# Delta-rule attention, Mish block and Sinkhorn experts on one core: block 0 solved by 16x16 triangles with TensorE products, block 1 solved on VectorE late in the Mish units

## The chip, the cores and the metric

One NeuronCore of a Trainium2 chip runs the whole program. The metric is the device time of one execution in microseconds (us), the median of several runs. All times below are us unless marked ns. TensorE (PE) multiplies, VectorE (DVE), ScalarE (ACT) and GpSimd (POOL) work element by element, SyncE (SP) issues the transfers.

## The reference

Three stages follow one another; `_moe_ref` and `_moe2_ref` are a Mish block and eight experts.

```python
for t in range(S):                                  # S = 768, batch 4, 8 heads, D = 48
    kt, vt, bt = (k_n[:, :, t], v[:, :, t], beta[:, :, t, None])
    y[:, :, t] = np.einsum('bhd,bhde->bhe', q[:, :, t], state)
    v_old = np.einsum('bhde,bhd->bhe', state, kt)
    state = state + bt[:, :, :, None] * np.einsum('bhd,bhe->bhde', kt, vt - v_old)
...
h = x @ w_in; sp = log1p(exp(h)); g = h * tanh(sp); x = g @ w_out      # d_ff = 2048
...
P = exp(x @ w_gate - max)                           # then 8 Sinkhorn rounds over rows and columns
out += P[:, e:e + 1] * (np.maximum(x @ w1[e], 0.0) @ w2[e])            # e = 0..7, F = 1024
```

## The kernel before, in words

The sequence is cut into 6 blocks of 128 steps (`NBLK`), each block into two chunks of 64. Inside a chunk the recurrence is a triangular system: with G the masked product of the keys among themselves, every head needs the inverse of a unit triangular 64x64 matrix. The kernel inverts the two 32x32 diagonal triangles of each and joins them with TensorE products:

- `st_gk`, `st_gq`, `st_g` (lines 988 to 1035) multiply keys with keys and keys with queries. `mask_g` and `causal` mask what `st_g` copied out unmasked.
- `lane_in_one` or `lane_in_ops` turns the triangles by 32x32 transposes into the tile `lane`, where every partition holds a triangle of its own; `elim_ops` (line 1075) eliminates there in 30 steps, each one product (line 1083) and one addition (line 1089) on up to 240 elements of a partition. `st_lane_out` (line 1097) transposes the result twice, into `t11` and `diag`.
- `st_place`, `st_m1` and `st_m2` put the inverted triangles back into `gx` and make the 32x32 corner between them, by 64 products each.
- The chain of the block is then `st_z`, `st_w`, `st_s`, `st_y` for each of its two chunks, two at a time; `st_x1` transposes its result into the input of the Mish block.

Before the first Mish unit there is a head: all of this for block 0, with nothing to hide it, and the raw products of block 1. Then come the windows, one for a block: 16 Mish units, and in windows 0 and 1 the 8 units of expert 0 after them. Mish unit f is `m_first` (9 products of 512 columns, line 300), Mish on ACT (`m_a`, line 1289), a split into a high and a low part (`m_c`; the low part `gl` on DVE, line 1299) and `m_second` (9 products, line 1310). A bank that `m_first` wrote is free again when `gl` has been made. In window 0 the weights are also decoded from 64-bit numbers: a transfer (`fetch`, lines 167 and 171), a scaling on ACT (line 206), three instructions on DVE (lines 189, 192, 197), a split on ACT (line 260) and a subtraction on DVE (line 262) for each unit; the transfer for unit i+4 is issued when unit i is converted, and a copy of each converted unit is stored to memory.

The order on every engine is the order of the program text (`manual_schedule`). What stands beside which unit comes from the table `PLACES`: for block c+1 the mark at which its solve must be finished (`drain_elim`, `st_lane_out`; `st_m1` follows one mark later, `st_place` and `st_m2` two), the marks of its chain stages; and for block c+2 the marks of its norms, masks, `st_g` and the start of its solve. Marks 0 to 15 are the Mish units, 16 to 19 the end of the Mish part (f1 to f4), 20 to 27 expert 0. `fill(us)` takes solve steps worth so many planned us from the queue `eq` after each unit.

Block 0 is solved in the head by all 60 instructions of `elim_ops`. Block 1's solve begins at the end of the head: 18 instructions on POOL (`elim1(18, nc.gpsimd)`), the other 42 on DVE beside Mish units 3 to 11, and its chain stands at marks 14 to 22.

Of the kernel before, what the change touches and what calls it, by code (L numbers as in the profile page):

```python
# [84 lines left out]
def delta_mish_sinkhorn_kernel(  # L85
# [691 lines left out]
    def o_store():  # L777

        u, half, t = todo.popleft()
        if t < 0:  # L780
            f, x, (n, d) = fin[u], slice(512 * half, 512 * half + 512), divmod(~t, KD)
            tt(out=f[:, d, x], in0=f[:, d, x], in1=f[:, 3 + 3 * n + d, x], op=ALU.add)
            return
            return True
        o_write(u, half, t, o_turn(u, half, t, (0, 1, 2)))

    todo = deque()
# [8 lines left out]
    if True:  # L796
# [9 lines left out]
        lane = ap_p.tile([128, 32, 32], F32, name="lane")  # L806
# [22 lines left out]
        def gx(c):  # L829
            return gxs[c % 2]  # L830
# [236 lines left out]
        def lane_in_one(c):  # L1067
            v = gx(c).rearrange("p t h x -> p x (t h)")
            return [
                (1.94, lambda: nc.vector.transpose(out=lane, in_=v[:, 0:32, :])),  # L1070
                (0.09, lambda: nc.vector.memset(lane.rearrange("p t i -> p (t i)")[:, 0:1024:33], 1.0)),
                (0.0, lambda: diag_clear(c)),
            ]

        def elim_ops(c, eng=(nc.vector,)):
            ops = []
            for s in range(1, 31):
                n = 31 - s
# [278 lines left out]
        with tc.manual_schedule():  # L1357
# [44 lines left out]
            for _, op in lane_in_one(0):  # L1402
                op()
            e0 = [op for _, op in elim_ops(0)]

            def el(n):
                for _ in range(n):
                    e0.pop(0)()
# [9 lines left out]
            banks[:] = [0, [A1, A1, (ps_o1, "o0")]]  # L1418
            for t in range(4):
                run(*[lambda hf=hf: st_g(1, t, hf, False) for hf in range(2)])  # L1420
            for n in range(4):
                begin_decode(n)
            el(len(e0) - 24)
            nc.vector.memset(mi_f[1][:, 0:1], 0.0)
            warm(12, i=1)
            el(len(e0))
            st_lane_out(0)

# [4 lines left out]
            def elim1(n, eng):
                elim_eng[0] = eng
                for _ in range(min(n, len(ops1))):
                    ops1.popleft()[1]()
# [9 lines left out]
            for op in norm_ops(1, ALL):
                op()
            for t in range(4):
                prep_mb(1, t, nc.gpsimd)
            for t in range(4):  # L1450
                mask_g(1, t, nc.gpsimd)
# [7 lines left out]
            for t in range(2, 4):  # L1459
                prep_v_act(0, t)  # L1460
            s0[0]()
            s0[1]()
            converts(1)
            z1 = [st_z(0, t) for t in range(2, 4)]
            z1[0]()
            gq[0]()
            z1[1]()
            gq[1]()
            run(*[lambda t=t: st_y(0, t) for t in range(2)])
            for n in range(4, 6):  # L1470
                fetch(n)
            for t in range(4):
                diag_left(1, t)
            in1 = [op for _, op in lane_in_one(1)]
            elim_eng = [nc.gpsimd]
            ops1 = deque(elim_ops(1, elim_eng))
            dec(2)
            wb = [st_w(0, t) for t in range(2, 4)]
            gq[2]()
            wb[0]()  # L1480
            gq[3]()
            wb[1]()
            run(*[lambda t=t: st_y(0, t) for t in range(2, 4)])
            for n in range(6, 8):
                fetch(n)
# [26 lines left out]
        def drain_decode():  # L1512
# [11 lines left out]
        def window(c):  # L1524
# [53 lines left out]
        with tc.manual_schedule():  # L1578
            banks[:] = [0, [A1, A1]]
            for c in range(NBLK):  # L1580
# [36 lines left out]
                for f in range(U1 + (3 if c < NE0 else 2)):  # L1617
# [240 lines left out]
```

## Time and profile before

| what | us |
| --- | --- |
| median of 3 runs | 2233.88 |
| the runs | 2229.70, 2234.07, 2233.88 |
| the profiled execution, its own time | 2229.53 |
| span of its trace, first to last instruction | 2227.7 |
| mean granted clock of TensorE in it | 0.978 of 2.4 GHz |

The span leaves 1.8 us outside the trace. All starts below count from the start of the span. In the views a line such as `L1083` is a line of the kernel before; `x64` counts instructions, and an fp32 product counts as two of them (two passes); what stands in brackets is how long the engine stood idle before, and what ended it.

### The profile page before, as it was taken

Reading aid. Unit: us, or ns where it says so; the run is one execution under the profiler, and the core shown is the slowest. Engines: PE = TensorE matmul, PEld = TensorE weight load, DVE = VectorE, ACT = ScalarE, POOL = GpSimd, SP = SyncE. Lnnn points to the kernel's source line nnn. Section 1 sums busy time; section 2 is a strip of 40 time slices with the busy share of each in tenths; the row PEclk is TensorE's granted clock in tenths of the full one; section 3 lists DMA queues with packets and bytes.
Section 4 is the critical chain, followed back from the end, with each engine's and each line's share of the span. In section 5 each row is a group of like instructions: output and inputs, shape, how many; then the busy total and the mean of one; then the engine's idle time right before and its main releaser. Section 6 shows DMA issues by size and latency. Waiting matters only on the chain.

```text
span 2227.7 us, 34746 instructions
## 1 busy us (share of the span) xinstructions
PE 2165.4 (97%) x14133; PEld 1792.0 (80%) x14133; DVE 1394.4 (63%) x2289; ACT 691.9 (31%) x1212; POOL 673.6 (30%) x528
## 2 busy tenths in 40 slices
PE   7889898999999999999999999999999999999999
PEld 6668787888888788888888888888888888888887
DVE  8894726473821276777776776666666666666665
ACT  6453332333324445233333322112212121211122
POOL 3504441435324656677878600000000000000000
PEclk7799999999999999999999999999999999999999
DMA  6576733544446446655555444444443454444441
GB/s 185 184 245 202 232 124 133 191 165 154 143 143 207 161 156 221 233 195 199 202 195 197 153 143 155 150 148 161 138 161 124 150 154 158 137 147 147 165 151 43
DMA packets 123648, 370.35 MB, mean 166 GB/s; under 512 B 9440, under 2 KB 51232, under 8 KB 123232
## 3 DMA queue, kind: packets, MB, share of 16 engines
q1 hardware_dynamic: 122912, 367.74, 48.3%
q8 instruction: 111, 1.82, 0.3%
q10 hardware_dynamic: 576, 0.39, 0.1%
q14 instruction: 49, 0.40, 0.1%
HBM read 274.15 MB, written 93.95 MB: 165 GB/s over the span
## 4 chain that ended last, share of the span: by engine, by line
PE 86%; DVE 8%; issue 2%; DMA 1%; POOL 1%; ACT 1%; SPq 0%; DVEq 0%; POOLq 0%; ACTq 0%
PE s L663 33%; PE b L596 31%; PE psh L300 7%; PE x L1310 6%; DVE t L1083 1%; DVE lane L1089 1%; PE y L324 1%; PE psa L1020 1%; DVE us L876 1%; PE psa L1168 1%; DVE lane L1053 1%; PE psa L1126 1%; PE psa L1141 1%; PE psa L1224 1%; PE psa L1190 1%
## 5 line engine op out<-in xcount | busy, mean ns | idle before, releaser
L596 PE MATMUL b<-gx,gw 128*128 128x512 f32 x3036 | 795.5, 390 | 0.1
L603 DVE TENSOR_TENSOR gt<-b,gt 128x512 f32<-128x512 f32 x644 | 436.0, 689 | 460.8 <-PE b L596 429.5
L596 PEld LDWEIGHTS b<-gx,gw 128*128 128x128 f32 x3036 | 568.5, 188 | 118.6 <-ACT gt L605 0.9
L663 PE MATMUL s<-gh,gw 128*128 128x512 f32 x2208 | 622.7, 390 | 0.6 <-DVE gy L706 0.4
L638 ACT ACTIVATE gh<-gt 128x512 fp32r<-128x512 f32 x368 | 232.8, 633 | 933.5 <-DVE gt L632 926.1
L663 PEld LDWEIGHTS s<-gh,gw 128*128 128x128 f32 x2208 | 413.6, 188 | 87.0 <-DVE gy L706 0.8
L663 PE MATMUL s<-gl,gw 128*128 128x512 f32 x1104 | 326.8, 390 | 0.0
L632 DVE SCALAR_TENSOR_TENSOR gt<-gt,gp 128x512 f32<-128x512 f32 x336 | 277.0, 825 | 4.5
L300 PE MATMUL psh<-x,w 128*128 128x512 f32 x1008 | 262.0, 405 | 11.8 <-DVE gl L1299 10.1
L663 PEld LDWEIGHTS s<-gl,gw 128*128 128x128 f32 x1104 | 206.8, 188 | 42.8
L300 PEld LDWEIGHTS psh<-x,w 128*128 128x128 f32 x1008 | 188.2, 192 | 59.8 <-DVE gl L1299 9.5
L641 POOL TENSOR_TENSOR gl<-gt,gh 128x512 fp32r<-128x512 f32 x128 | 186.3, 1462 | 77.4 <-ACT gh L638 72.3
L641 DVE TENSOR_TENSOR gl<-gt,gh 128x512 fp32r<-128x512 f32 x240 | 164.5, 686 | 37.0 <-ACT gh L638 36.8
L1299 POOL TENSOR_TENSOR gl<-x,gh 128x512 fp32r<-128x512 f32 x80 | 103.0, 1288 | 256.1 <-ACT gh L1297 238.5
L536 POOL TENSOR_TENSOR gx<-gxr,gx 128x768 fp32r<-128x768 f32 x18 | 33.3, 1847 | 407.0 <-ACT gx L535 407.0
L1310 PE MATMUL x<-gh,w 128*128 128x512 f32 x576 | 155.3, 406 | 0.0
L467 POOL TENSOR_TENSOR gw<-gr,gw 128x640 fp32r<-128x640 f32 x70 | 117.5, 1680 | 68.2 <-ACT gw L477 66.4
L1310 PEld LDWEIGHTS x<-gh,w 128*128 128x128 f32 x576 | 109.4, 194 | 24.0 <-issue 1.4
L1291 ACT ACTIVATE x<-psh 128x512 f32<-128x512 f32 x80 | 47.7, 596 | 132.3 <-PE psh L300 123.3
L1310 PE MATMUL x<-gl,w 128*128 128x512 f32 x288 | 82.8, 396 | 2.3 <-POOL gl L1299 2.3
L467 POOL TENSOR_TENSOR gw<-raw,gw 128x384 fp32r<-128x384 f32 x70 | 73.3, 1068 | 7.3 <-ACT gw L499 7.3
L984 POOL TENSOR_TENSOR kq<-kq,mask_sb 64x256 f32<-64x256 f32 (+1 forms) x72 | 58.6, 814 | 55.0 <-ACT kq L979 51.2
(203 smaller groups left out, 1984.8 us busy)
## 6 DMA issues: line engine op xcount, KB each, us to landing
gw<-wg SPq DMA_DIRECT2D x57, 1280.0 KB, 8.1
w<-wd SPq DMA_DIRECT2D x88, 768.0 KB, 4.4
gw<-wg SPq DMA_DIRECT2D x57, 768.0 KB, 5.1
wg<-gw SPq DMA_DIRECT2D x29, 1280.0 KB, 6.0
wg<-gw SPq DMA_DIRECT2D x29, 768.0 KB, 5.3
wd<-w SPq DMA_DIRECT2D x24, 768.0 KB, 5.7
gr<-in_w_dram SPq DMA_DIRECT2D x35, 384.0 KB, 3.2
raw<-in_w_dram SPq DMA_DIRECT2D x35, 384.0 KB, 3.8
```

What stands on the lines that cost most here:

```text
L300: mm(ps, lhsT=wi(u, pw, kc), rhs=(xh, xl)[px][:, kc, :], start=(n == 0), stop=(n == 3 * KD - 1))
L467: nc.gpsimd.tensor_tensor(out=w[:, 1, lo:hi], in0=r, in1=w[:, 0, lo:hi].bitcast(F32), op=ALU.subtract)
L596: mm(ps, lhsT=w[:, pw, i * 128:i * 128 + 128], rhs=x[:, px, j, :], start=(n == 0), stop=(n == last))
L603: add = lambda o, i: nc.vector.tensor_tensor(out=t[:, o], in0=ps, in1=t[:, i], op=ALU.add)
L632: nc.vector.scalar_tensor_tensor(out=t, in0=t, scalar=0.0, in1=pbs[u, e][:, o:o + 512], op0=ALU.max, op1=ALU.mult)
L638: nc.scalar.activation(out=h, in_=t, func=AF.Copy)
L641: return lambda: eng.tensor_tensor(out=l, in0=t, in1=h.bitcast(F32), op=ALU.subtract)
L663: mm(o[k], lhsT=w[:, pw, at:at + 128], rhs=hids[s, z][ph], start=(start and new and n == 0), stop=(end and not new and n == 2))
L984: nc.gpsimd.tensor_tensor(out=o, in0=o, in1=mask_sb[p, None, :].to_broadcast([64, hs.stop - hs.start, CH]), op=ALU.mult)
L1291: nc.scalar.activation(out=mi_x[u % 2], in_=hps.pop(u), func=AF.Mish)
L1299: eng.tensor_tensor(out=l, in0=p, in1=h.bitcast(F32), op=ALU.subtract)
L1310: mm(x2ps[c][k], lhsT=wo(u, pw, k * 128, k * 128 + 128), rhs=(h, l)[pg], start=(f == 0 and n == 0), stop=(f == U1 - 1 and n == 2))
```

## The change

- Block 0: `half_ops` eliminates the 16x16 diagonal triangles of each 32x32 triangle, both in one instruction (`lane2` is a view of them), 14 steps of two instructions on 28 to 112 elements, after POOL has cleared the square between them. `st_e16` and `st_o16` make that square by TensorE products with 16 rows and 16 columns (128 products, then 192), with ACT copies and six DVE additions between and behind them.
- The raw products of block 1 (`raw_g`, one call for half the heads of a 64-step chunk) no longer stand before block 0's inverse, but in eight pieces between the stages of its chain. The masked copies of `st_gq` (DVE) move ahead of the chain, `diag_left(1, t)` on ACT behind it.
- Block 1 is solved wholly on DVE: queued at Mish unit 11, 0.6 us of fill up to there and 3.4 from unit 12 on, finished at mark 17; its chain stands at marks 20 to 27, beside expert 0. Block 2's solve is queued at mark 27 instead of 26, one mask at 24 instead of 23 and the last at 25 instead of 24.

```diff
+        lanes = ap_p.tile([128, 1056], F32, name="lane")
+        lane = lanes[:, 0:1024].rearrange("p (t i) -> p t i", i=32)
+        lane2 = lanes.rearrange("p (k m) -> p k m", k=2)[:, :, 0:512].rearrange("p k (t i) -> p k t i", i=32)
...
+        def half_ops(c):
+            t = t11.rearrange("p b i -> p (b i)")
+            ops = [(0.0, lambda: nc.gpsimd.memset(lane[:, 16:32, 0:16], 0.0))]
+            for s in range(1, 15):
+                n = 15 - s
+                p = t[:, 0:2 * n * s].rearrange("p (k n s) -> p k n s", k=2, s=s)
...
+                        out=p, in0=lane2[:, :, s + 1:16, s:s + 1].to_broadcast([128, 2, n, s]),
+                        in1=lane2[:, :, s:s + 1, 0:s].to_broadcast([128, 2, n, s]), op=ALU.mult,
...
+        def st_e16(c, hf):
...
+                    mm(ps[p:p + 32, i], lhsT=g[p:p + 16, t, h, o:o + 32], rhs=t11[p:p + 16, t * H + h, :],
+                       start=True, stop=True)
+            return lambda: nc.scalar.activation(out=em(hf), in_=ps, func=AF.Copy, scale=low16)
+        def st_o16(c, hf):
...
+                    mm(ps[q, 0, i], lhsT=diag[q, b, :], rhs=e[q, i, 0:16], start=True, stop=True)
...
+                    mm(ps[q, 1, i], lhsT=e[q, i, :], rhs=diag[q, b, 16:32], start=True, stop=True)
...
-            for t in range(4):
-                run(*[lambda hf=hf: st_g(1, t, hf, False) for hf in range(2)])
...
+            raw_g((0, 0))
+            el(12)
             nc.vector.memset(mi_f[1][:, 0:1], 0.0)
-            warm(12, i=1)
+            warm(10, i=1)
             el(len(e0))
             st_lane_out(0)
...
+            ea, eb = st_e16(0, 0), st_e16(0, 1)
+            ea()
+            eb()
+            gq[0]()
+            oa, ob = st_o16(0, 0), st_o16(0, 1)
...
+            raw_g((0, 1))
...
+            oa()
+            gq[3]()
+            ob()
             m1a = m_run(st_m1(0, 0, (32,)))
...
-            elim1(18, nc.gpsimd)
...
-            (11, two(14, 15, 17, 18, 19, 20, 21, 22), 16, [21, 22, 23, 24], two(23, 24, 25, 26), 18, 26, 26),
+            (17, two(20, 21, 22, 23, 24, 25, 26, 27), 16, [21, 22, 24, 25], two(23, 24, 25, 26), 18, 26, 27),
...
-                rest["s3"].append(lambda: eq.extend(ops1))
+                rest["s11"].append(lambda: eq.extend(elim_ops(1)))
...
-                    fill(1.2 if not c else 3.2 if c >= NE0 and f > 8 else 2.0)
+                    fill((0.6 if f < 12 else 3.4) if not c else 3.2 if c >= NE0 and f > 8 else 2.0)
```

Three places show the new order. The first is ACT at the end of the head, where block 0's result `yd` becomes the Mish input `x`. Before:

```order
L1226 ACTIVATE yd<-psa 128x384 x2
L1061 ACTIVATE gx_153<-gx_153 32x8x32 x8
L1226 ACTIVATE yd<-psa 128x384 x2
L260 ACTIVATE w_90<-bits_174 128x768
L1234 ACTIVATE x_1107<-psa 128x512 x3
```

and with the change (lines of the changed kernel: 1286 is `st_y`, 981 the copies of `st_g`, 1063 `diag_left`, 1294 `st_x1`):

```order
L1286 ACTIVATE yd<-psa 128x384 x2
L981 ACTIVATE gx_153<-psa 128x256
L981 ACTIVATE kq_147<-psa 64x256 x2
L981 ACTIVATE gx_153<-psa 128x256
L981 ACTIVATE kq_147<-psa 64x256 x2
L206 ACTIVATE xr<-xr 128x768
L206 ACTIVATE bits_175<-bits_175 128x768
L1286 ACTIVATE yd<-psa 128x384 x2
L1063 ACTIVATE gx_153<-gx_153 32x8x32 x8
L260 ACTIVATE w_90<-bits_174 128x768
L1294 ACTIVATE x_1409<-psa 128x512 x3
```

The eight copies of `diag_left` moved from between the two pairs of `yd` to behind the last one, and copies of block 1 and two scalings moved in between.

The second is DVE in a Mish unit of window 0 (`gl` is line 1299, `lane` and `t` are the solve). Before, one unit late in the decoding:

```order
L1299 TENSOR_TENSOR gl<-psh,gh 128x512
L1089 TENSOR_TENSOR lane<-lane,t_167 128x11x20
L1083 TENSOR_TENSOR t_167<-lane 128x210
L1089 TENSOR_TENSOR lane<-lane,t_167 128x10x21
L189 TENSOR_SCALAR kq_141<-kq_141 128x768
L192 SCALAR_TENSOR_TENSOR kq_141<-kq_141 128x768
L197 SCALAR_TENSOR_TENSOR kq_141<-kq_141 128x768
L262 TENSOR_TENSOR w_89<-kq_140,w_89 128x768
```

With the change the same unit runs from its `gl` straight into the decoding, and the solve (lines 1085 and 1091) begins behind the `gl` of unit 10:

```order
L1359 TENSOR_TENSOR gl<-psh,gh 128x512
L1085 TENSOR_TENSOR t_167<-lane 128x30
L1091 TENSOR_TENSOR lane<-lane,t_167 128x30
L1085 TENSOR_TENSOR t_167<-lane 128x58
L189 TENSOR_SCALAR kq_142<-kq_142 128x768
L192 SCALAR_TENSOR_TENSOR kq_142<-kq_142 128x768
L197 SCALAR_TENSOR_TENSOR kq_142<-kq_142 128x768
L262 TENSOR_TENSOR w_90<-kq_141,w_90 128x768
L1359 TENSOR_TENSOR gl<-psh,gh 128x512
L1091 TENSOR_TENSOR lane<-lane,t_167 128x29x2
```

Eleven solve instructions follow this second `gl` (unit 11), then nine, eight, eight and nine behind those of units 12 to 15, and the rest among the last steps of the Mish part; 42 had stood beside units 3 to 11 before.

The third is PE where block 1's inverse is used (`gx_153`). Before, `st_m1` stood between the first products of unit 13 and the second ones of unit 11:

```order
L300 MATMUL psh<-x_1107,w_89 128x512 x2
L300 MATMUL psh<-x_1108,w_89 128x512
L1126 MATMUL psa<-t_167,gx_153 32x32 x64
L1310 MATMUL x_1255<-gh,w_93 128x512
L1310 MATMUL x_1256<-gh,w_93 128x512
```

With the change it follows the second products of the last unit, 15, and nothing stands between (1186 is `st_m1`, 1201 `st_m2`, 1228 and 1229 `st_z`):

```order
L1370 MATMUL x_1540<-gl,w_92 128x512
L1370 MATMUL x_1541<-gl,w_92 128x512
L1186 MATMUL psa<-t_167,gx_153 32x32 x64
L1201 MATMUL psa<-yd,mb_176 32x32 x32
L1201 MATMUL psa<-yd,mb_177 32x32 x32
L1228 MATMUL psa<-us_162,kq_144 64x48
L1229 MATMUL psa<-us_162,kq_144 64x48
```

`st_m1`, `st_m2` and the first chain stage moved as one piece from among the Mish units to between them and expert 0.

## Rows read from the trace of the kernel before

**Rows 1.** The page: busy shares, and the chain that ended last by engine.

```profile
PE 2165.4 (97%) x14133; PEld 1792.0 (80%) x14133; DVE 1394.4 (63%) x2289; ACT 691.9 (31%) x1212; POOL 673.6 (30%) x528
PE 86%; DVE 8%; issue 2%; DMA 1%; POOL 1%; ACT 1%; SPq 0%; DVEq 0%; POOLq 0%; ACTq 0%
```

**Rows 2.** By stretch: length, PE, PEld, DVE, ACT, POOL, PEclk, DMA share, GB/s.

```profile
39.82:79.12 39.30, 31.83 (x657) 29.40 (x657) 33.15 (x44) 19.44 (x45) 21.91 (x18) 0.57 0.27 84
79.12:105.98 26.86, 21.63 (x138) 16.32 (x136) 25.16 (x35) 13.13 (x19) 15.22 (x20) 0.87 0.55 203
105.98:141.72 35.74, 30.79 (x127) 23.11 (x127) 34.77 (x57) 19.76 (x28) 0.00 (x0) 1.00 0.87 296
141.72:193.70 51.98, 43.56 (x730) 37.05 (x730) 36.44 (x62) 21.53 (x36) 13.89 (x6) 0.85 0.60 190
193.70:244.48 50.78, 48.55 (x451) 42.83 (x449) 26.43 (x52) 16.03 (x32) 28.29 (x30) 0.99 0.63 231
```

**Rows 3.** Timeline of DVE: block 0's solve (start, duration, instruction).

```profile
17.89 0.17 DVE L1083 TENSOR_TENSOR t<-lane 128x30 f32<-128x30 f32 x1
20.02 0.29 DVE L1083 TENSOR_TENSOR t<-lane 128x130 f32<-128x130 f32 x1
...
39.82 2.09 DVE L1098 STREAM_TRANSPOSE t<-lane 128x1024 f32<-128x1024 f32 x1
```

**Rows 4.** Groups of PE, 45.38 to 47.3: `st_m1` and `st_m2` interleaved.

```profile
L1141 PE MATMUL psa<-yd,mb 32*32 32x32 f32 x62 | 1.9, 237 | 0.4 <-DVE mb L876 0.4
L1126 PE MATMUL psa<-t,gx 32*32 32x32 f32 x60 | 1.8, 237 | 0.0
```

**Rows 5.** Timeline of ACT in the head.

```profile
28.32 0.76 ACT L979 ACTIVATE kq<-psa 64x256 f32<-64x256 f32 x2
...
67.57 3.42 ACT L1061 ACTIVATE gx<-gx 32x256 f32<-32x256 f32 x8
...
75.37 0.49 ACT L1226 ACTIVATE yd<-psa 128x384 f32<-128x384 f32 x1 [2.12 <-PE psa L1225]
```

**Rows 6.** Timeline of DVE: masked copies of `st_gq`, low parts of `st_x1`.

```profile
70.75 1.41 DVE L1006 TENSOR_TENSOR kq<-psa,mask_sb 64x512 f32<-64x512 f32 x2
...
79.28 1.89 DVE L876 TENSOR_TENSOR x<-psa,x 128x512 fp32r<-128x512 f32 x3
```

**Rows 7.** Timeline of DVE beside unit 3: a subtraction, and the solve's first step.

```profile
97.72 1.29 DVE L262 TENSOR_TENSOR w<-kq,w 128x768 fp32r<-128x768 f32 x1
...
100.80 0.38 DVE L1083 TENSOR_TENSOR t<-lane 128x210 f32<-128x210 f32 x1 [1.19 <-POOL lane L1089]
```

**Rows 8.** Groups of DVE, 105.98 to 141.72, seven units (count, sum, mean ns).

```profile
L262 DVE TENSOR_TENSOR w<-kq,w 128x768 fp32r<-128x768 f32 x7 | 6.7, 952 | 0.0
L1299 DVE TENSOR_TENSOR gl<-psh,gh 128x512 fp32r<-128x512 f32 x7 | 4.8, 683 | 0.0
...
L1083 DVE TENSOR_TENSOR t<-lane 128x228 f32<-128x228 f32 (+6 forms) x11 | 4.3, 393 | 0.2
```

**Rows 9.** Timelines of SP and ACT: a unit's transfer issued, and its scaling.

```profile
110.45 0.38 SPq L167 DMA_DIRECT2D kq<-in_w_in_dram  x1
...
117.64 0.93 ACT L206 ACTIVATE kq<-kq 128x768 f32<-128x768 f32 x1 [2.00 <-DMA kq<-in_w_out_dram]
```

**Rows 10.** Timeline of PE: waits of `st_m1` and of a chain stage.

```profile
149.52 2.68 PE L1126 MATMUL psa<-t,gx 32*32 32x32 f32 x93 [5.47 <-DVE t L1098]
...
197.76 0.21 PE L1208 MATMUL psa<-us,kt 64*48 64x48 f32 x1 [1.07 <-DVE us L876]
...
275.40 1.83 PE L1126 MATMUL psa<-t,gx 32*32 32x32 f32 x61 [4.53 <-DVE t L1098]
```

**Rows 11.** Groups of PE, 163.9 to 182: chain stages of block 1.

```profile
L1190 PE MATMUL psa<-r,gx 64*64 64x48 f32 x64 | 2.1, 219 | 0.0
L1168 PE MATMUL psa<-us,kq 48*64 48x48 f32 x32 | 2.1, 219 | 0.0
L1208 PE MATMUL psa<-us,kt 64*48 64x48 f32 x32 | 1.6, 206 | 0.0
```

More of the change, by code (lines that the diff above doesn't have):

```diff
@@ L328, in delta_mish_sinkhorn_kernel @@
     gate = const.tile([128, 192], F32, name="gate")
+    low16 = gate[:, 132:133]
     sk = {}
@@ L783, in o_store @@
             return
-            return True
         o_write(u, half, t, o_turn(u, half, t, (0, 1, 2)))
@@ new lines, in st_e16 @@
+        def st_e16(c, hf):
+            ps = bank().rearrange("p (b i) -> p b i", i=32)
+            g = gx(c)
+            for i in range(16):
+                t, h = 2 * hf + i // H, i % H
+                for p in range(0, 128, 32):
+                    o = p % 64
+                    mm(ps[p:p + 32, i], lhsT=g[p:p + 16, t, h, o:o + 32], rhs=t11[p:p + 16, t * H + h, :],
+                       start=True, stop=True)
+            return lambda: nc.scalar.activation(out=em(hf), in_=ps, func=AF.Copy, scale=low16)
@@ new lines, in st_o16, with post @@
+        def st_o16(c, hf):
+            ps = bank().rearrange("p (w b i) -> p w b i", w=2, i=16)
+            e = em(hf)
+            for i in range(16):
+                b = 16 * hf + i
+                for p in (0, 64):
+                    q = slice(p, p + 32)
+                    mm(ps[q, 0, i], lhsT=diag[q, b, :], rhs=e[q, i, 0:16], start=True, stop=True)
+            for i in range(16):
+                b = 16 * hf + i
+                for p in range(0, 128, 32):
+                    q = slice(p, p + 32)
+                    mm(ps[q, 1, i], lhsT=e[q, i, :], rhs=diag[q, b, 16:32], start=True, stop=True)
+            bs = slice(16 * hf, 16 * hf + 16)
+            def post():
+                for p in (0, 64):
+                    x = t11[p:p + 32, bs, 0:16]
+                    vec.tensor_tensor(out=x, in0=x, in1=ps[p:p + 32, 0], op=ALU.add)
+                x = diag[:, bs, 16:32]
+                vec.tensor_tensor(out=x, in0=x, in1=ps[:, 1], op=ALU.add)
+            return post
@@ L1401, in delta_mish_sinkhorn_kernel @@
                 diag_left(0, t)
-            for _, op in lane_in_one(0):
-                op()
-            e0 = [op for _, op in elim_ops(0)]
+            in0 = [op for _, op in lane_in_one(0)]
+            e0 = [op for _, op in half_ops(0)]
+            for op in in0[0:2] + e0[0:1] + in0[2:]:
+                op()
+            e0 = e0[1:]
+            m = [mask_sb[:, x:x + 1] for x in (16, 32, 48)]
+            nc.gpsimd.tensor_tensor(out=low16, in0=m[1], in1=m[0], op=ALU.subtract)
+            nc.gpsimd.tensor_tensor(out=low16, in0=low16, in1=m[2], op=ALU.subtract)
+            nc.gpsimd.tensor_scalar(out=low16, in0=low16, scalar1=1.0, scalar2=None, op0=ALU.add)
             def el(n):
@@ L1417, in delta_mish_sinkhorn_kernel, with raw_g @@
             gq = [st_gq(0, t, True) for t in range(4)]
-            banks[:] = [0, [A1, A1, (ps_o1, "o0")]]
-            for t in range(4):
-                run(*[lambda hf=hf: st_g(1, t, hf, False) for hf in range(2)])
-            for n in range(4):
-                begin_decode(n)
-            el(len(e0) - 24)
+            CHAIN, SIDE = [A1, A1], [(ps_o1, "o0")]
+            def raw_g(*parts):
+                banks[:] = [0, SIDE]
+                for t, hf in parts:
+                    st_g(1, t, hf, False)()
+                banks[:] = [0, CHAIN]
+            raw_g((0, 0))
+            el(12)
             nc.vector.memset(mi_f[1][:, 0:1], 0.0)
-            warm(12, i=1)
+            warm(10, i=1)
             el(len(e0))
@@ L1431, in dec @@
                     dq.popleft()[1]()
[L1433 to L1436, printed above, removed]
+            banks[:] = [0, CHAIN]
+            ea, eb = st_e16(0, 0), st_e16(0, 1)
[3 more added lines that the diff above has]
+            oa, ob = st_o16(0, 0), st_o16(0, 1)
+            SIDE = [(ps_o1, "o0"), (ps_h, "h"), (ps_h, "h")]
+            CHAIN = [A1, A1, (ps_o1, "o1"), (ps_o1, "o2")]
+            raw_g((0, 1))
+            for op in norm_ops(1, ALL):
+                op()
+            for t in range(4):
+                prep_mb(1, t, nc.gpsimd)
+            gq[1]()
+            gq[2]()
+            begin_decode(0)
+            begin_decode(1)
+            oa()
+            gq[3]()
+            ob()
             m1a = m_run(st_m1(0, 0, (32,)))
@@ L1445, in delta_mish_sinkhorn_kernel @@
             wa = [st_w(0, t) for t in range(2)]
[L1446 to L1451, printed above, removed]
+            raw_g((1, 0), (1, 1))
             for p in wa:
@@ L1458, in delta_mish_sinkhorn_kernel @@
             m2b[0]()
-            for t in range(2, 4):
-                prep_v_act(0, t)
+            raw_g((2, 0), (2, 1))
+            prep_v_act(0, 2)
             s0[0]()
             s0[1]()
-            converts(1)
             z1 = [st_z(0, t) for t in range(2, 4)]
             z1[0]()
-            gq[0]()
+            converts(1)
+            prep_v_act(0, 3)
             z1[1]()
-            gq[1]()
             run(*[lambda t=t: st_y(0, t) for t in range(2)])
             for n in range(4, 6):
+                fetch(n)
+            raw_g((3, 0), (3, 1))
+            for t in range(4):
+                mask_g(1, t, nc.gpsimd)
+            begin_decode(2)
+            begin_decode(3)
+            dec(2)
+            wb = [st_w(0, t) for t in range(2, 4)]
+            wb[0]()
+            wb[1]()
+            run(*[lambda t=t: st_y(0, t) for t in range(2, 4)])
+            for n in range(6, 8):
                 fetch(n)
@@ L1474, in delta_mish_sinkhorn_kernel @@
             in1 = [op for _, op in lane_in_one(1)]
[L1475 to L1485, printed above, removed]
             decodes(2)
@@ L1497, in delta_mish_sinkhorn_kernel @@
             converts(3)
-            elim1(18, nc.gpsimd)
             decodes(4)
             converts(4)
-            elim_eng[0] = nc.vector
             wslots.append(late_p.tile([128, 2, 2, DM], F32R, tag="e2", name=f"w{NS1 - 1}"))
```

10 lines of the change are left out of this document (9 added, 1 removed).

## The prediction

> **What bounds the kernel now.** First the page: TensorE is busy 97% of the span and carries 86% of the chain that ended last [rows 1]. No work of TensorE is saved (the change adds products), so a gain must come from places where TensorE waits. Next the table by stretch [rows 2]; the change reaches from the head to the first unit of window 1.
> - Head, 39.82 to 79.12: granted clock 0.57 of 2.4 GHz, so mostly 1.2 GHz, DVE busy 33.15 of 39.30. It is a chain of small steps. Its front is block 0's solve, 17.89 to 39.82 on DVE [rows 3].
> - Units 0 to 4, 79.12 to 105.98: DVE busy 25.16 of 26.86, at one point waiting 1.19 for POOL's part of block 1's solve [rows 7].
> - Seven units, 105.98 to 141.72: 5.10 each, DVE busy 34.77 of 35.74, TensorE 30.79. DVE is the bound.
> - 141.72 to 193.70: `st_m1` waits 5.47 for the solve [rows 10].
> - Expert 0, 193.70 to 244.48: TensorE busy 48.55 of 50.78. What is added here is paid.
>
> **The change, part by part** (negative is a gain).
>
> *S1, head.* The short solve has 28 instructions of 28 to 112 elements. Rows of 30 and 130 elements took 0.17 and 0.29 [rows 3]; at 0.28 it is 7.8 against 21.9. The first transposition (2.09) ends at 27.9 instead of 41.9, 14.0 earlier. On this path come `st_e16`, a copy, `st_o16` and additions. A product is two passes. With passes in four row groups, 122 took 1.9, some 15 ns each at 1.2 GHz [rows 4]; in two groups 93 took 2.68, 29 ns [rows 10]. `st_e16`: 256 passes, 3.8. `st_o16`: 384 passes, 128 of them in two groups, 7.5 on its own, 3.8 if the two sorts overlap; taken 5.0, since its second half covers the first half's additions. ACT's copy 0.7, the last additions 1.3, `st_m1` 1.8: it ends at 40.4. Before it began behind the transposition's end at 41.9 and ended about 2.1 later at 44.0. So 3.6 of the 14.0 are left.
>
> The rule against this part: the Trainium skill ("TensorEngine Tiling (Array Packing)", Instruction Overhead) gives each matmul a fixed cost of about 60 cycles and says that one with a free size of 1 lasts as long as one with 60, so 16 columns would be no cheaper than 48. By its figure 640 passes would be an estimated 16 at 2.4 GHz and 32 at 1.2 GHz. Rows 4 disagree as far as groups overlap; where they don't, rival R3 prices it.
>
> Behind `st_m1` three more things change on the chain. DVE's masked copies of `st_gq` are gone from it: 1.41 a pair [rows 6], four pairs, of which three stood between the additions of the chain, 4.2. The eight copies of `diag_left` come in: they ran at 67.57 for 3.42 while the chain was on TensorE (ACT waited 2.12 for it before the last copy of `yd`, which ended at 75.86 [rows 5]); now they stand between that copy and `x`. So with nothing else DVE's low parts of `x`, 79.28 before [rows 6], start 3.6 + 4.2 - 3.4 = 4.4 earlier, at 74.9. Against this, six calls of `raw_g` put three copies each into ACT's queue inside the chain, 0.38 a copy (two in 0.76 [rows 5]), 1.1 a call. With all six on the path it is 81.5. I take two calls, 77.1, because ACT was busy only 19.44 of the 39.30 [rows 2]: **-2.2** (bounds -4.4 and +2.2).
>
> *S2, units 0 to 4.* POOL's 18 instructions are gone, with them DVE's wait of 1.19 and three solve steps of 0.38 behind it [rows 7]. While POOL worked, decode instructions were longer: 1.29 for a subtraction [rows 7] that has a mean of 0.952 later [rows 8]; over the unit's four about 1.2. **-3.5** (bounds -2.4, the wait and steps alone, and -3.6).
>
> *S3, seven units.* 11 solve products at 0.393 [rows 8] and 11 additions as long leave: 8.6 of 35.74. DVE alone would then need 3.9 per unit. Next comes the transfers' bound: their share was 0.87 at 5.10 per unit [rows 2], at a share of 1.0 that is 4.44; issue to scaling is 7.2 [rows 9] over four units in flight, below that. So 4.45 per unit: **-4.6** (bounds -3.5 and -6.0, the last if TensorE's and the transfers' slack carries over from units 0 to 4).
>
> *S4, from unit 10's `gl` to expert 0's first product*, 51.98 before. Now DVE sets it: the solve's 60 instructions 21.9 (as block 0's [rows 3]); two units at 3.9, a third's subtraction and `gl` 0.95 + 0.68, two more `gl` 1.4 [rows 8]: 10.8; two sums, three low parts and a copy, six operations as wide as the three in 1.89 [rows 6], 3.8; the transposition 2.1 [rows 3]. 38.6. Then TensorE alone: `st_m1` 3.7 (128 passes at 29 ns), `st_m2` as many 3.7, `st_z` 3.0 (between 2.1 [rows 11] and twice that). 49.0: **-3.0**. The wait before `st_m1` of 5.47 goes, but a longer one takes its place: the last unit's `m_second` ends some 10.7 before the transposition does, with nothing queued between.
>
> *S5, expert 0.* What leaves the Mish part comes here: two `st_w` 2.1 each, `st_s` 1.6, `st_y` and `st_z` about 2.1 each [rows 11], 10.0, and TensorE has only 2.2 idle there. **+7.8**: the idle time goes first, the rest lengthens the stretch.
>
> *S6, window 1.* Block 2's solve is queued one mark later, one fill of 3.6 fewer before its `st_m1`, which waited 4.53 already [rows 10]. **+3.2** (bounds +2.2 and +4.0: the longer expert part gives DVE a little back).
>
> No other work covers S5 or S6. DMA instructions are the same in number; `fetch` of units 4 to 7 moves by a few instructions on SP, ahead of nothing that waits. POOL, freed of the solve in units 0 to 4, gives nothing else.
>
> Sum: -2.2 - 3.5 - 4.6 - 3.0 + 7.8 + 3.2 = **-2.3**. The profiled execution took 2229.53, so it would take 2227.2. That execution is 4.4 below the median of 2233.88; the four shown have a mean of 2231.8, which I take as the level: 2231.8 - 2.3 = **2229.5**. A measurement of this kernel tells 0.2%, 4.5, from no change.
>
> **The rivals.**
> - *R1, the head gains more.* If the denser products of block 0 bring the granted clock of the head to 2.4 GHz, `st_e16`, `st_o16` and `st_m1` halve, 3.1 more, and S6 ends at +2.2: sum -6.4, 2225.4; with no copy of ACT on the path (2.2) and S3 at its best (1.4) down to -10.0, 2221.8. For it: the clock is 1.00 in the dense units. Against it: 0.57 in the head, 0.85 around `st_m1` [rows 2].
> - *R2, slower.* In expert 0 the stages of the chain and `st_g` share two PSUM banks (`banks` is set to `A1` twice). A pair of stages can only start when both banks have been copied out: 0.49 a copy [rows 5], about 1.0 a pair; a stage waited 1.07 for DVE there before [rows 10]. The chain's 16 products and the marks of `st_g` (21, 22, 24, 25) make about 11 hand-overs. If expert 0's products don't cover them: +11, sum +8.7, 2240.5. It decides from 0.62 each (11 x 0.62 = 6.8 puts the sum over 4.5). Against it: each mark has expert products of over a microsecond behind it.
> - *R3, slower.* Passes of 16 columns cost as those of 48, 33 ns (2.1 for 64 [rows 11]), without overlap of groups: 640 x 33 ns = 21.1 against 8.8, +12.3, sum +10.0, 2241.8. Against it: rows 4.
> - *R4, no change.* Five of the six `raw_g` calls fall on the chain: 74.9 + 5.5 = 80.4, S1 +1.1, sum +1.0, 2232.8. For it: the pieces stand directly ahead of the copies that the chain needs.
>
> That the change does not do what it says is excluded by the order shown: the solve has left units 3 to 9, `st_m1` stands behind unit 15.
>
> **How the numbers follow.** Chances: forecast 0.35 (of it 0.13 faster, 0.21 no change, 0.01 slower; its own range -9 to +3, 2223 to 2235), R1 0.32 (0.29 and 0.03), R2 0.17 (0.02 no change, 0.15 slower), R3 0.05, R4 0.11 (0.10 and 0.01). Faster 0.42, no change 0.36, slower 0.22. The range: below, R1's far end less the 2.2 by which single executions lie off their mean, 2219.6; above, R3's 2241.8. What it leaves out is R2 with longer hand-overs, and cases below R1.
>
> **What would show it.** Right: block 0's first transposition starts near 25.8 and its `st_m1` ends at 37 to 41; the low parts of `x` start near 77; `gl` of units 5 to 10 follow at 4.4 to 4.5 with a DMA share near 1; TensorE idles about 11 before block 1's `st_m1`; expert 0's stretch is 58 to 59 with TensorE busy nearly throughout; window 1's `st_m1` waits near 8. Wrong: the low parts of `x` later than 79.3 (R4, or R3 if `st_o16` alone takes 10 or more); units at 5 (then DVE was not the bound); waits of 0.6 or more at each pair in expert 0 (R2).

## The result and the profile after

The changed kernel took 2253.03 (median of 4 runs, 2251.38 to 2255.48) against 2231.79 before (4 runs): ratio 1.0096, 95% interval 1.0078 to 1.0115. It is 21 slower; the forecast was 2229.5, and the range given ended at 2241.8. The profiled execution took 2251.80, its span is 2250.0 against 2227.7.

The page of the changed kernel, lines as in [rows 1]:

```profile
PE 2167.7 (96%) x14771; PEld 1795.0 (80%) x14771; DVE 1392.0 (62%) x2281; ACT 692.6 (31%) x1214; POOL 659.4 (29%) x514
PE 87%; DVE 6%; issue 1%; DMA 1%; POOL 1%; ACT 1%; SPq 0%; DVEq 0%; ACTq 0%; POOLq 0%
```

TensorE's busy time is 2.3 higher than before; the other 20 of the longer span are idle. The table by stretch of the changed kernel has the columns of [rows 2]. The stretches run from block 0's first transposition to the low parts of `x`, to `gl` of unit 3, to the end of `gl` of unit 10, to expert 0's first product, to window 1's first.

```profile
26.02:90.29 64.27, 42.49 (x1414) 38.25 (x1412) 35.15 (x50) 34.22 (x85) 24.36 (x19) 0.73 0.38 127
90.29:113.34 23.05, 19.53 (x122) 15.49 (x123) 21.85 (x29) 11.02 (x16) 1.89 (x2) 0.78 0.48 160
113.34:144.36 31.02, 31.02 (x139) 25.68 (x138) 28.04 (x38) 19.75 (x29) 0.00 (x0) 1.00 1.01 367
144.36:198.32 53.96, 34.42 (x414) 28.68 (x412) 49.48 (x95) 20.81 (x35) 15.44 (x7) 0.79 0.57 186
198.32:258.34 60.02, 60.02 (x771) 52.94 (x769) 29.24 (x53) 17.02 (x34) 26.34 (x28) 0.96 0.52 190
```

Read against before, the ledger of the prediction becomes:

| step | forecast | measured | from |
| --- | --- | --- | --- |
| S1 head, to the low parts of `x` | -2.2 | +11.0 | 79.28 to 90.29 |
| S2 units to 3 | -3.5 | -2.9 | 25.98 to 23.05 |
| S3 seven units | -4.6 | -5.4 | 35.72 to 30.33 |
| S4 to expert 0 | -3.0 | +1.9 | 52.72 to 54.65 |
| S5 and S6, to window 1's `st_m1` | +11.0 | +12.4 | 81.70 to 94.05 |
| sum, at that `st_m1` | -2.3 | +17.0 | 275.40 to 292.37 |

(S3 and S4 meet at the start of unit 10's `gl`, 140.98 and 143.67.) Two steps carry the miss: S1 by 13.2, S4 by 4.9. At the end of this execution it is 22.3 instead of 17.0. Set beside each other product by product, the two traces place the other 5: the later windows add 0.8 (their `st_m1` are 17.2 to 17.8 late), 2.4 come between 746 and 784, where two of the last Mish units' first products wait 1.06 and 2.21 for their weights (before, one waited 1.24), 0.7 come among the first experts, and 1.4 behind the last expert product. Why the weights landed later is not shown, and single executions differ by 2 to 4.

**Where S1 went.** DVE of the changed kernel: the first transposition (start, duration), the last addition of the square, the low parts of `x`.

```profile
26.02 2.07 DVE L1158 STREAM_TRANSPOSE t<-lane 128x1024 f32<-128x1024 f32 x1
...
48.27 0.42 DVE L878 TENSOR_TENSOR yd<-yd,psa 128x256 f32<-128x256 f32 x1
...
90.29 1.89 DVE L878 TENSOR_TENSOR x<-psa,x 128x512 fp32r<-128x512 f32 x3
```

The short solve did what was forecast: its transposition starts at 26.02 instead of 39.82. But then 20.6 pass from the transposition's end (28.09) until the last addition ends at 48.69, where about 11 were forecast. TensorE in between (1129 is `st_e16`, 1140 and 1145 the two sorts of `st_o16`; shown is the first piece, and each piece behind a pause):

```profile
28.14 1.71 PE L1129 MATMUL psa<-t,gx 16*32 16x32 f32 x176 [1.27 <-DVE t L1158]
34.92 1.29 PE L1129 MATMUL psa<-t,gx 16*32 16x32 f32 x80 [5.06 <-issue]
39.08 0.55 PE L1140 MATMUL psa<-mb,yd 32*32 32x16 f32 x14 [1.64 <-issue]
42.53 0.42 PE L1145 MATMUL psa<-yd,mb 32*32 32x16 f32 x17 [1.35 <-issue]
46.08 1.30 PE L1145 MATMUL psa<-yd,mb 32*32 32x16 f32 x81 [0.80 <-issue]
```

TensorE stops four times, 8.85 in all, for "issue": it waits for nothing that the profile shows, no tile and no bank. From the first pause on the pieces come at 34.92, 39.08, 42.53, 46.08, some 3.5 to 4.2 apart.

**Where S4 went.** DVE and POOL beside unit 12 of the changed kernel (1085 and 1091 are the solve, 262 on POOL the subtractions for expert 0's first weights, 986 masks of block 1's keys):

```profile
156.53 0.35 DVE L1091 TENSOR_TENSOR lane<-lane,t 128x184 f32<-128x184 f32 x1
156.91 1.90 DVE L1085 TENSOR_TENSOR t<-lane 128x198 f32<-128x198 f32 x1
158.84 3.11 DVE L1091 TENSOR_TENSOR lane<-lane,t 128x198 f32<-128x198 f32 x1
161.99 1.32 DVE L1085 TENSOR_TENSOR t<-lane 128x210 f32<-128x210 f32 x1
163.34 1.86 DVE L1091 TENSOR_TENSOR lane<-lane,t 128x210 f32<-128x210 f32 x1
165.24 0.39 DVE L1085 TENSOR_TENSOR t<-lane 128x220 f32<-128x220 f32 x1
```

```profile
156.58 2.00 POOL L262 TENSOR_TENSOR w<-raw,w 128x768 fp32r<-128x768 f32 x1 [59.62 <-DVE t L1085]
158.55 1.40 POOL L986 TENSOR_TENSOR kq<-kq,mask_sb 64x512 f32<-64x512 f32 x1
159.92 1.81 POOL L262 TENSOR_TENSOR w<-raw,w 128x768 fp32r<-128x768 f32 x1
161.81 1.27 POOL L986 TENSOR_TENSOR kq<-kq,mask_sb 64x512 f32<-64x512 f32 x1
163.15 1.81 POOL L262 TENSOR_TENSOR w<-raw,w 128x768 fp32r<-128x768 f32 x1
```

Four steps take 8.19 instead of some 1.5, while POOL works: 6.7 lost. By these rows each of the four ends 0.2 behind the end of one of POOL's operations (158.81, 161.95, 163.31, 165.20 against 158.58, 161.73, 163.08, 164.96; POOL's times are rough). TensorE's waits for the inverse are 9.27 and, in window 1, 8.01 (5.47 and 4.53 in [rows 10]):

```profile
187.77 3.46 PE L1186 MATMUL psa<-t,gx 32*32 32x32 f32 x122 [9.27 <-DVE t L1158]
...
292.37 0.85 PE L1186 MATMUL psa<-t,gx 32*32 32x32 f32 x24 [8.01 <-DVE t L1158]
```

### The profile page after: what moved, and what is told of

Its sections match the earlier page's. It is cut to its first block, busy times and chain, and to the rows that moved or that the text cites. A ratio compares the mean times of both kernels' runs of the same rounds, so it can differ in the third digit from the quotient of the medians.

```text
span 2250.0 us, 35994 instructions
## 1 busy us (share of the span) xinstructions
PE 2167.7 (96%) x14771; PEld 1795.0 (80%) x14771; DVE 1392.0 (62%) x2281; ACT 692.6 (31%) x1214; POOL 659.4 (29%) x514
## 4 chain that ended last, share of the span: by engine, by line
PE 87%; DVE 6%; issue 1%; DMA 1%; POOL 1%; ACT 1%; SPq 0%; DVEq 0%; ACTq 0%; POOLq 0%
PE s L664 33%; PE b L597 30%; PE psh L300 8%; PE x L1370 6%; PE y L324 2%; DVE t L1085 1%; DVE lane L1091 1%; PE psa L1022 1%; PE psa L1228 1%; PE psa L1284 1%; PE psa L1250 1%; DVE us L878 1%; PE psa L1186 1%; PE psa L1201 1%; DMA kq<-in_w_out_dram 1%
```

## The experiments

Landmarks of the executions (us from the span's start): T block 0's first transposition, X low parts of `x`, U3 and U10 `gl` of those units, B block 1's first transposition, E expert 0's first product, M block 2's `st_m1`. T alone moves by 4 between executions with the same head (before, and e2, e8, e11, e12), so stretches are compared, not starts.

| run | T | X | U3 | U10 | B | E | M |
| --- | --- | --- | --- | --- | --- | --- | --- |
| before | 39.82 | 79.28 | 105.26 | 140.98 | 147.35 | 193.70 | 275.40 |
| changed | 26.02 | 90.29 | 113.34 | 143.67 | 185.67 | 198.32 | 292.37 |
| e1_old_block1 | 26.02 | 91.11 | 117.48 | 153.21 | 159.59 | 205.84 | 287.49 |
| e2_old_head | 43.91 | 83.35 | 105.48 | 136.29 | 178.28 | 190.96 | 284.86 |
| e4_sub_dve | 26.39 | 90.02 | 113.11 | 143.67 | 181.57 | 194.22 | 287.99 |
| e8_pool36 | 40.51 | 79.22 | 103.73 | 140.90 | 143.95 | 189.72 | 271.59 |
| e11_repaired2 | 40.20 | 79.61 | 101.73 | 132.19 | 170.07 | 182.78 | 274.94 |
| e12_pool24 | 43.39 | 82.84 | 107.32 | 139.22 | 169.92 | 186.27 | 277.18 |

### The two halves apart

From the changed kernel, block 1 put back:

```diff
-            (17, two(20, 21, 22, 23, 24, 25, 26, 27), 16, [21, 22, 24, 25], two(23, 24, 25, 26), 18, 26, 27),
+            (11, two(14, 15, 17, 18, 19, 20, 21, 22), 16, [21, 22, 23, 24], two(23, 24, 25, 26), 18, 26, 26),
...
+            ops1 = deque(elim_ops(1, elim_eng))
+            for _ in range(18):
+                ops1.popleft()[1]()
```

> The new head (block 0 by 16x16 triangles) alone; block 1 solved and placed as before (18 steps on GpSimd, 42 on VectorE beside Mish units 3 to 11, chain at marks 14 to 22). Theory H (the head lost the time: its x came 11.0 later, 79.28 to 90.29): x's low parts again start near 90, the rest follows as before, so about 11 over before, 2240 to 2247. Rival W (what was moved in window 0 lost it): within 4.5 of before, 2227 to 2236.

From the kernel before, the opposite: the new row of `PLACES`, the solve queued at unit 11, no steps on GpSimd.

> Block 0 solved as before; block 1 as in the change (VectorE from unit 11, chain beside expert 0). Ledger of the changed run without its head: units 0 to 4 -2.9, seven units -5.4, to expert 0 +1.9, expert 0 +9.2, window 1 +3.1, sum +5.9: about 2237.7 (2235 to 2241). Theory H holds if this is the smaller part; if rival W holds it is 15 or more over before, 2247 or later.

Measured: the new head alone 2247.09, ratio 1.0070 (1.0053 to 1.0086), 0.1 above what theory H gave; X is 91.11 and the 12 stay to M (287.49 against 275.40). The new block 1 alone 2236.11, ratio 1.0025 (1.0016 to 1.0035): 5.6, where its ledger gave 5.9; W falls. The halves, 16.5 and 5.6, add up to the whole (21 to 22). So the head lost most, and within block 1's part the gains of S2 and S3 (X to U10 52.94 instead of 61.70) are outweighed by U10 to M (148.57 instead of 134.42).

### What stops TensorE in the 16-row products

```diff
+        hold_t = const.tile([1, 16], F32, name="hold_t")
...
-            for n in range(4):
-                fetch(n)
+            fetch(0)
...
             oa()
             gq[3]()
             ob()
+            nc.sync.dma_start(out=hold_t, in_=t11[0:1, 31, 0:16])
+            for n in range(1, 4):
+                fetch(n)
+            load_vt(1)
...
```

> The change, with the transfers of weights 1 to 3 and of block 1's values held back until block 0's inverse is done, and unit 1's scaling after them. Theory S (TensorE ran out of instructions, and loading them took 5.1 because the queues were full with weights from 27 to 37): the idle of 5.06 inside the 16-row products falls below 2, the three shorter ones (1.64, 1.35, 0.80) stay, as they came with idle queues; x's low parts start at 84 to 87 instead of 90.3. Rival P (the products wait for their banks or for rows of the transposition): the idle of 5 stays where it is.

The long pause fell only to 3.70, and the others came as 1.07, 1.35, 0.80: between the theories. The low parts of `x` came at 92.41, not at 84 to 87. The queues had not been free, though: block 1's keys and queries and weight 0 filled them up to 32. (The whole time of this one execution, 2290.84, says nothing on this: see the last section.) So in the next kernel (e5) all of them were held, with a copy into a spare part of an existing tile:

> The change, with all transfers that block 0's inverse does not need (three quarters of block 1's keys and queries, weights 0 to 3, block 1's values) held back until it is done, and the scalings of units 0 and 1 after them. In the run held before, the long idle of TensorE was 3.7 instead of 5.1, with queues busy up to 32. Theory S (instruction loading held up by full queues): the long idle falls below 2, and the first pause comes no earlier. Rival L (the loading of instructions is slow by itself, some 155 products' passes per 3.5): a pause of 3 or more stays with idle queues.

TensorE of that run, from the first product to the last additions' pieces:

```profile
28.42 2.00 PE L1129 MATMUL psa<-t,gx 16*32 16x32 f32 x176 [1.33 <-DVE t L1158]
32.17 1.29 PE L1129 MATMUL psa<-t,gx 16*32 16x32 f32 x80 [1.76 <-issue]
35.77 0.55 PE L1140 MATMUL psa<-mb,yd 32*32 32x16 f32 x14 [1.07 <-issue]
39.50 0.41 PE L1145 MATMUL psa<-yd,mb 32*32 32x16 f32 x17 [1.62 <-issue]
43.05 1.30 PE L1145 MATMUL psa<-yd,mb 32*32 32x16 f32 x81 [0.80 <-issue]
```

What the DMA queues moved from 26 to 48 in the changed run, and from 26 to 46 in this one, in 40 slices each:

```profile
GB/s 214 285 367 385 367 365 382 371 369 372 391 378 352 374 388 421 412 381 389 210 39 12 0 0 0 30 0 0 0 0 0 0 30 0 0 0 0 0 30 0
GB/s 0 0 0 0 0 0 0 33 0 0 0 0 0 0 33 0 0 0 0 0 0 33 0 0 0 0 0 0 0 33 0 0 0 0 0 0 33 0 0 0
q8 instruction: 5, 0.08, 1.7%
```

The queues are full up to 37 in the changed run; here they carry nothing but five loads of instructions (`q8`). The first pause fell from 5.06 to 1.76, at the same place (after 176 passes): S holds for 3.3 of it. L's sign, a pause of 3 or more, did not show, but with idle queues four pauses of 0.8 to 1.8 stay, the pieces 3.6 to 3.7 apart, so full queues are not the whole cause. The whole was no faster (2252.02, one execution): the inverse was done 3.0 earlier, but X came at 92.79. Scalings on ACT were moved behind the inverse together with the weights, and VectorE's decoding, which stands ahead of the chain's copies, waited 3.94 and 2.76 for them:

```profile
64.27 0.96 DVE L192 SCALAR_TENSOR_TENSOR bits<-bits 128x768 int32<-128x768 int32 x1 [3.94 <-ACT bits L206]
```

Next (e6) the products were doubled, and then (e10) the instructions halved at equal columns; each diff shows one of the edited places:

```diff
...
-                    mm(ps[q, 0, i], lhsT=diag[q, b, :], rhs=e[q, i, 0:16], start=True, stop=True)
+                    for _ in range(2):
+                        mm(ps[q, 0, i], lhsT=diag[q, b, :], rhs=e[q, i, 0:16], start=True, stop=True)
...
```

> The change, with every product of the two 16-row stages issued twice into the same place (640 more passes). Theory L (TensorE gets about 155 passes of instructions per 3.5, that is 23 ns a pass): the last additions of the inverse (48.27 in the changed run) come 14 to 15 later, with four more pauses. Rival E (the passes cost what the engine takes, 15 ns by the rows of four groups): 9 to 10 later, and no more pauses than before.

```diff
...
-            for i in range(16):
+            for i in range(0, 16, 2):
...
-                    mm(ps[q, 1, i], lhsT=e[q, i, :], rhs=diag[q, b, 16:32], start=True, stop=True)
+                    mm(ps[q, 1, i:i + 2], lhsT=e[q, i, :], rhs=diag[q, b:b + 2, 16:32], start=True, stop=True)
```

> The change, with one product for two heads in both 16-row stages: half the instructions, as many columns. It leaves out the second head's own factor, so these products are not the reference's. Theory L (TensorE waits for instructions, 28 ns a pass from the doubled run): 320 passes fewer, the last additions of the inverse 7 to 9 earlier than 48.7 (counted from a transposition that starts at 26.0), pauses at most half. Rival E (time goes by columns): less than 2 earlier.

Doubled: from the transposition's start to the end of the last addition 40.31 (29.38 to 69.69) instead of 22.67, 17.6 for 640 passes, 27.6 ns a pass, with nine pauses. Halved: 15.44 (26.21 to 41.65), 7.2 less with two pauses (3.72 and 2.35), and X at 83.31 instead of 90.29; the whole times, one execution each, were 2269.39 and 2243.49. So the time goes by instructions, not by columns, and E falls both times. L's price was low for the doubled run (14 to 15 and four more pauses; it was 17.6 and five more). In the doubled run, three pieces on TensorE and, from 42 to 66, what the DMA queues carried:

```profile
38.36 2.00 PE L1130 MATMUL psa<-t,gx 16*32 16x32 f32 x128 [4.44 <-issue]
42.37 2.00 PE L1130 MATMUL psa<-t,gx 16*32 16x32 f32 x128 [2.00 <-issue]
45.82 1.31 PE L1130 MATMUL psa<-t,gx 16*32 16x32 f32 x78 [1.45 <-issue]
```

```profile
GB/s 0 0 27 0 0 0 0 0 27 0 0 0 0 0 27 0 0 0 0 27 0 0 0 0 0 0 27 0 0 0 0 0 27 0 0 0 0 27 0 0
q8 instruction: 7, 0.11, 1.9%
```

128 passes run in 2.00 (15.6 ns each, the 15 ns that the forecast took from [rows 4]), then TensorE stops. In these 24 us nothing moved but seven loads of instructions, 0.11 MB, 16 KB each, one every 3.5. One load for 128 passes is 128 bytes a pass. The Trainium skill ("Perfetto Trace Analysis", The 4-stage abstract model) gives an instruction 64 bytes; a pass here is two instructions, a weight load and a product, so the trace agrees. Where the passes run at 15.6 ns, the engine works 2.0 and stands dry for 1.5 to 2.0 behind them.

The loads of the whole program bear this out. The page's row of instruction loads before, changed, doubled, halved:

```profile
q8 instruction: 111, 1.82, 0.3%
q8 instruction: 116, 1.90, 0.3%
q8 instruction: 121, 1.98, 0.3%
q8 instruction: 114, 1.87, 0.3%
```

The change adds 638 passes on TensorE by the page and five loads, the doubling 640 passes and five more, the halving takes 320 passes and two loads away: some 128 passes a load.

### What else stood in the head's chain

```diff
...
-            raw_g((0, 1))
...
-            raw_g((1, 0), (1, 1))
+            raw_g((0, 1), (1, 0), (1, 1))
+            begin_decode(0)
+            begin_decode(1)
...
             run(*[lambda kc=kc: st_x1(0, kc) for kc in range(KD)])
+            for t in range(4):
+                diag_left(1, t)
```

> The change, with three things moved out of the head's chain: the second piece of block 1's raw products behind block 0's corner products, the scalings of units 0 and 1 behind those too, and the eight copies of block 1's left halves behind x. Theory Q (what stands ahead in TensorE's and ScalarE's queues delays the chain: 2.0 for the raw products, 1.5 for the scalings, 3.4 for the copies): x's low parts start 5 to 7 earlier than 90.3, at 83 to 85. Rival: other limits take over, less than 3 earlier.

X came at 92.19, 1.9 later than in the changed run, whole time 2252.59 (one execution). Q falls. DVE and TensorE of this run where the gain went:

```profile
65.58 1.98 DVE L192 SCALAR_TENSOR_TENSOR bits<-bits 128x768 int32<-128x768 int32 x1 [8.10 <-ACT bits L206]
```

```profile
68.86 1.92 PE L1201 MATMUL psa<-yd,mb 32*32 32x32 f32 x64 [5.52 <-DVE us L878]
```

A decoding instruction now stands on DVE ahead of the chain's `us` and waits 8.10 for the moved scaling, and TensorE waits 5.52 for `us`. The three moves can't be valued apart from this run; where the 2.9 go that the changed head loses behind its corner products (34.9 from their end to X, 32.0 before) stays open.

### Block 1's part

```diff
-        eng = nc.vector if kind(i) == "wide" else nc.gpsimd
+        eng = nc.vector if kind(i) == "wide" or i < U1 + 3 else nc.gpsimd
```

> The change, with the three subtractions of expert 0's first weights on VectorE instead of GpSimd. Theory G (VectorE's solve steps are held up while GpSimd works: four steps of 198 and 210 elements took 1.3 to 3.1 instead of 0.37, just while GpSimd made three subtractions and two masks): at most two steps over 1 remain (beside the two masks), and block 1's first transposition comes 2 to 5 earlier counted from x's low parts (95.4 after them in the changed run). Rival: the steps of that size are slow by themselves: all four stay, and the transposition comes about 3 later.

```profile
156.92 0.37 DVE L1085 TENSOR_TENSOR t<-lane 128x198 f32<-128x198 f32 x1
157.32 0.37 DVE L1091 TENSOR_TENSOR lane<-lane,t 128x198 f32<-128x198 f32 x1
157.72 0.38 DVE L1085 TENSOR_TENSOR t<-lane 128x210 f32<-128x210 f32 x1
158.14 0.38 DVE L1091 TENSOR_TENSOR lane<-lane,t 128x210 f32<-128x210 f32 x1
```

POOL in this run, the first operation after 97:

```profile
186.24 5.43 POOL L927 TENSOR_TENSOR ne<-ss,half_sb 128x32 f32<-128x32 f32 x1 [89.50 <-DVE ss L911]
```

The same steps take 0.37 and 0.38. All four are short, since POOL does nothing beside them: the masks, too, ran earlier once no subtraction stood ahead of them. X to B is 91.55 instead of 95.38, 3.8 less, which is the 6.7 lost to POOL's company less three subtractions of 0.95 that DVE now makes; 2245.28 in one execution. G holds. The Trainium skill ("GPSIMD Engine Reference", Specifications) says that GpSimd shares its SBUF interfaces with VectorE, and that VectorE's instructions with two SBUF inputs contend with it. The solve's steps have two such inputs, and the trace agrees: beside POOL they took up to eight times their length (3.11 for 0.37).

> Block 0 as before, block 1 as in the change, with two terms of its ledger taken out: the three subtractions on VectorE (3.8 measured) and block 2's solve queued at mark 26 as before (3.1 expected, the fill that was lost). From the old head's run, 2236.1: about 2229 (2226 to 2233), within 4.5 of before. Rival: the two gains are behind other limits (expert 0's stretch sets the time): no less than 2233.5.

It took 2229.30, ratio 1.0001 (0.9988 to 1.0013). In this kernel block 2's triangles are turned (230.52) before the last masked copy of its products is in (232.65), so half the heads of its last chunk are solved from unfinished data. The next one queues the solve behind those copies and is else the same:

> As the run repaired before, with block 2's solve queued behind the last masked products of the same mark, so that it reads them all. Block 1's move costs as much as it gains once the two terms are out: within 2 of the run repaired before, 2229.3, and within 4.5 of the kernel before.

2230.12, ratio 1.0002 (0.9993 to 1.0012) against before. Without POOL's company and the lost fill, block 1's move is even: from X to U10 it gains 9.1 (52.58 instead of 61.70), from U10 to M it pays 8.3 back (142.75 instead of 134.42), as block 1's chain then stands beside expert 0, where TensorE had 2.2 idle [rows 2].

### Two versions that start from what was learned

> As e11, with the first 24 of block 1's 60 solve steps on GpSimd at the end of the head, where it is idle in that version until unit 12. Theory V (the wait of TensorE of some 10 before block 1's corner products is VectorE's solve): the transposition comes 7 to 9 earlier (24 steps of 0.34), GpSimd's company costs VectorE some 3 in units 1 to 5, sum -4 to -6 against e11: 2223 to 2226. Rival: the units' loss eats the gain, within 2 of e11.

2228.67 (2222.54 to 2235.80), 1.5 below e11 and ratio 0.9996 (0.9983 to 1.0008) against before: no change, the rival. U10 to B did fall, 30.70 instead of 37.88, as V had it. It was paid back: X to U10 3.8 more, and B to E 16.35 instead of 12.71, because `st_m2` stopped for instructions, here too:

```profile
180.94 1.82 PE L1141 MATMUL psa<-yd,mb 32*32 32x32 f32 x61 [3.47 <-issue]
```

The DMA queues were full up to 178 in this execution (146 to 269 GB/s); in e11 they carried nothing but loads of instructions from 173.5 to 182, and `st_m2` ran without a pause. That is theory S a second time, seen and not tried.

The kernel before with two numbers and a mark changed:

```diff
-            elim1(18, nc.gpsimd)
+            elim1(36, nc.gpsimd)
...
-                rest["s3"].append(lambda: eq.extend(ops1))
+                rest["s8"].append(lambda: eq.extend(ops1))
```

(and `fill(1.8` for `fill(1.2` in window 0.)

> The kernel before, with GpSimd doing 36 of the 60 steps of block 1's solve instead of 18, VectorE the last 24 beside units 8 to 11. From the ledger: VectorE loses the wait of 1.2 and three steps per unit in units 3 to 7, so 0.5 to 0.7 per unit where transfers bind at 4.4; the rest as before. 3 to 6 faster than before, 2225 to 2228. Rival: GpSimd's work slows VectorE's decoding (1.2 per unit in units 2 and 3 before) by as much as it saves: within 2 of before.

2226.49, ratio 0.9985 (0.9976 to 0.9995) against 2229.18: 2.7 faster than before, within the 2225 to 2228 expected, and the best version found, slightly. The reason expected did not hold, so the number was luck: U3 to U10 got longer, 37.17 instead of 35.72, as POOL slows VectorE's decoding (a subtraction there took 1206 ns in the mean instead of 952). The gain is at B, 3.4 earlier, where the wait of `st_m1` falls from 5.47 to 2.11:

```profile
146.11 3.09 PE L1126 MATMUL psa<-t,gx 32*32 32x32 f32 x128 [2.11 <-DVE t L1098]
```

## Why the prediction was wrong

- **S1 failed at the price of the 16-row products, `st_e16` 3.8 and `st_o16` 5.0.** The 15 ns a pass were right for passes in a row (128 in 2.00), but taken from 122 passes, fewer than one load of instructions; 640 passes need five loads, and the sum had no term for them. A pass cost 27.6 ns by the doubled run, and the first load 3.3 more for full queues. From the transposition's end to `st_m1` it took 21.1 instead of some 10.7: 10.4 of the miss of 13.2. The rest is 1.0 in the corner products (two scalings stood ahead of a copy on ACT, and TensorE waited 1.52 for it instead of 0.57) and 1.5 behind them, whose cause stays open.
- **R3 had nearly the price (33 ns, 21.1) and the wrong mechanism**: passes of 16 columns are not as dear as those of 48, they run at 15.6 ns and then wait. R3's sum of +10.0 fell short since S4 was wrong as well. By the Trainium skill's rule of a fixed cost ("TensorEngine Tiling (Array Packing)", Instruction Overhead, cited in S1) the 640 passes were an estimated 16 to 32, and the stretch of 20.6 lies within. The row of 128 passes in 2.00, at a granted clock of 0.50 of 2.4 GHz, disagrees with the rule as the reason: by it 128 passes one behind the other would take an estimated 6.4.
- **S4 failed at "the solve's 60 instructions 21.9".** That was the length of block 0's solve, with gaps, and no subtraction or mask of POOL lay beside that one. Here it was 28.2: 26.5 busy (14.1 and 12.4 below) and 1.7 of gaps. POOL's subtractions and masks beside four steps took 6.7 of it; without them the steps come to 19.8 busy, as block 0's did (19.9). The other terms of S4 came 1.4 lower together. [Rows 7] had shown POOL's company on a subtraction (1.29 for 0.95), and S2 counted it as a gain; the prediction did not ask what POOL does where the solve moves to.
- **S2, S3 and S6 were right, S5 nearly**: -2.9; -5.4 with a DMA share of 1.01; +9.2 for S5 (forecast +7.8), with TensorE busy 60.02 of 60.02 in expert 0; +3.1 for S6, with a wait of 8.01. In S3's stretch TensorE, too, was busy throughout (31.02 of 31.02), so whether the transfers alone set the unit, as S3 had it, is not shown. R2's hand-overs did not show. R1's clock did not come either: 0.60 of 2.4 GHz in the 16-row products.
- The last 5 of the 22.3, behind window 1's `st_m1`, were in no term of the sum; 2.4 of them lie where Mish units wait for weights, and the cause stays open.

Solve steps of the changed kernel as groups, 144 to 186:

```profile
L1091 DVE TENSOR_TENSOR lane<-lane,t 128x30 f32<-128x30 f32 (+14 forms) x30 | 14.1, 472 | 0.9
L1085 DVE TENSOR_TENSOR t<-lane 128x30 f32<-128x30 f32 (+14 forms) x30 | 12.4, 413 | 0.8
```

## What to carry to other kernels

Count instructions, not columns, where TensorE gets hundreds of small products in a row. In this case a stretch of up to 128 passes showed the engine's rate (15.6 ns), and 640 passes the rate at which instructions arrive (27.6 ns); a sum over hundreds has to use the second. Here even half the instructions did not make the exchange pay: X came at 83.31, 4.0 behind the kernel before. When work is moved beside other units, look up what GpSimd does there: the same steps took up to eight times as long.

## What the runs showed that was not expected

- In these runs TensorE's instructions came 16 KB at a time, one load every 3.5 to 3.7 with idle queues (128 of these passes), and the first one 3.3 later while weights filled the queues.
- POOL's company held four short steps of VectorE up to eight times as long, each until 0.2 behind the end of an operation of POOL.
- The first held run (e3) was 2290.84 in all, in one execution: TensorE's busy time rose to 2208.6 from 2167.7 in the changed run, and the mean of the experts' first products to 394 ns from 390. Besides the order, only one tile of 64 bytes and the transfer into it were added; whether the tile's place in memory did that was not tried. The next kernel used a spare part of an old tile and took 2252.02.
